# Two attention and gated-MLP layers on one core: engines held free ahead of the last chunks' chain, and the plan's price of narrow matmuls

## Chip, core and metric

One core of a Trainium2 chip. The kernel is one program; its time is the device time in microseconds of that core, as the median of several executions. The engines are TensorE (PE), VectorE (DVE), ScalarE (ACT), GpSimd (POOL) and SyncE (SP), each with its own instruction stream, which it works through in order, waiting on semaphores.

## What is computed

Two layers with the same weights over x of shape 2048 x 512, bfloat16:

```python
x = A_x
for _ in range(2):
    x = x + attention(layernorm(x))      # 32 heads of 16, one shared key and value head
    x = x + gated(layernorm(x))

# attention: q = x@wq (32 heads), k = x@wk, v = x@wv (16 columns each)
#            softmax(q k^T / 4) v, then @wo
# gated:     z = gelu(x@w_in)                      # 2048 x 1792
#            z1 = z[:, :896]; z2 = layernorm(z[:, 896:])
#            g = w_sp @ z2 + b_sp[:, None]         # w_sp is 2048 x 2048
#            (z1 * g) @ w_out
```

## The kernel before

**A plan made on the host.** The program is not written in the order in which it runs. Python code builds operations (`Op`: engine, duration in the plan, operations it depends on, priority) and a scheduler (`Sched`) plays them through in planned time; the order in which it commits them on each engine is the order of the instructions there. `_pick` chooses for an engine among the operations that are ready when it comes free, by priority; an operation that becomes ready a moment later is not considered, unless it comes from a stream with `grab`, which lets the engine stay idle for that long ahead of it. A result becomes visible some time after its end (`LAT`: 0.22 us from PE and ACT, 0.14 us from DVE, to readers on the same engine as well, except PE to PE). The waits of the program follow from the dependencies; nothing of the planned times is left in it but the order.

**Attention.** The 2048 queries come in chunks `[512, 512, 512, 256, 128, 128]` (`ci` 0 to 5). For each chunk and each set of four heads side by side there is a group of 16 units, one for each tile of 128 keys. A unit has four blocks of scores, 128 keys x 512. `FillStream` issues the score matmuls (qk, L1761) into PSUM in threes and twos by turns, `ExpStream` takes the exponential on ACT (L1428, output Pa, 128x1536 or 128x1024). A few blocks are computed on DVE instead (`DexStream`, L1615 to L1646, output Pd), in pairs of 1024. `SoloStream` places such a block by itself where PE would stand. `PVStream` multiplies with V (L1507). `WarmStream` issues matmuls on zeros (L1742) wherever the columns booked in the last 3.41 us of the plan fall below a bound; the columns of a job are its planned duration times a factor.

**The end of a chunk.** `finish_group` copies the group's result from PSUM (oT, L836), transposes it (for the last chunk on PE, else by DMA), takes the reciprocal of the softmax sums (L851) and normalises (on, L863). After the chunk's last group `project` transposes on, multiplies by wo (L943) and adds to X (L947). `mixer_chunk` takes the layer norm (st L638, mv L640, ve L642, POOL's rs L644, xn L653), transposes it (xnTB, L670 to L678), multiplies by w_in (L975 for the half z2, L1011 for z1), takes the gelu, and normalises z2 (st L1066, POOL's rs L1072, z2n L1076). Gelus are batched over chunks (0, 1), (2,), (3, 4), (5,), as ACT loads another table for them.

**The product with w_sp** runs over tiles of 128 rows s of z2 in passes: s 0 to 8 after chunk 1, 8 to 12 after chunk 2, 12 to 15 after chunk 4 (L1152 on PE, added up in gp by DVE, L1165). These jobs have low priority and fill gaps. The last tile, s = 15, is done after chunk 5 in `closing`: eight pieces of 256 rows; for each the product (L1211), a copy to E (DVE L1222 or ACT L1223), the addition of gp (L1226), the multiplication with z1 reloaded from DRAM (L1229), the product with w_out (L1244) and the addition to X (L1249). In layer 0 each piece is followed by the layer norm and the keys and values of layer 1, whose attention begins meanwhile; in layer 1 by the store.

**What a duration in the plan is.** `d_mm(n)` is the planned time of a matmul with n columns, `d_psum`, `d_sb` and `d_act` those of DVE and ACT operations. The lines that the change replaces:

```python
def d_mm(n):
    return max(n / 2400.0 + 0.006, min(0.045 + n * 0.43e-3, 0.155))
```

Of the kernel before, what the change touches and what calls it, by code (L numbers as in the profile page):

```python
# [6 lines left out]
BF16 = mybir.dt.bfloat16  # L7
# [25 lines left out]
class Op:  # L33
    __slots__ = ("eng", "fn", "dur", "deps", "prio", "seq", "start", "end", "vis", "sem", "val",
                 "clock", "unit", "job", "first", "nun", "users", "ready", "alts", "table", "lat", "dma", "at_commit", "cols", "slow")

# [21 lines left out]
class Sched:  # L58
# [3 lines left out]
    def __init__(self, side_banks):  # L62
        self.free = {e: 0.0 for e in ENGS}
        self.ready = {e: [] for e in ENGS}
        self.streams = {e: [] for e in ENGS}
        self.order = {e: [] for e in ENGS}
        self.commits = []
        self.banks = [Bank(b) for b in side_banks]
        self.seq = 0
        self.table = "exp"  # L70
        self.cache = {}
        self.nleft = 0
        self.exp_next = None
# [5 lines left out]
        self.full = False  # L79

    def lend(self, key, idxs, o):
# [34 lines left out]
    def op(self, eng, fn, dur, deps=(), prio=5.0, sem=None, job=None, first=False, alts=(), table=None,  # L116
           lat=None, dma=None, soft=(), cols=None, slow=None):
        o = Op()
        o.cols = dur * 2400.0 if cols is None else cols
        o.slow = dur * 2.0 if slow is None else slow  # L120
        o.eng = eng
        o.fn = fn
        o.dur = dur
        o.deps = []
        seen = set()
        for d in deps:
            if d is not None and id(d) not in seen:
# [24 lines left out]
        self.nleft += 1  # L152
        if o.nun == 0:
            self._arm(o)
        return o
# [13 lines left out]
    def _pick(self, eng):  # L169
# [3 lines left out]
        for o in self.ready[eng]:  # L173
            r = o.ready
            if o.first:
                r = max(r, bf)
            if o.eng != eng:
                dur = [d for e, _f, d in o.alts if e == eng][0]
                t0 = max(f, r)
                if self.exp_next is not None and self.exp_next() < t0 + dur:  # L180
                    continue
            if r < INF:
                late = o.unit is not None and o.unit < self.unit_now() + NEAR
                cands.append((r, 0.1 if late else o.prio, o.seq, o, 0.0))
        for st in self.streams[eng]:
# [98 lines left out]
    def job(self, pieces, cons, deps, prio, sem="side", piece_deps=None, soft=()):  # L284
# [3 lines left out]
        for i, (fn, dur) in enumerate(pieces):  # L288
            dd = list(deps) if i == 0 else [prev]
            if piece_deps is not None:  # L290
                dd += piece_deps[i]
            prev = self.op("pe", (lambda e, fn=fn: fn(e, j.bank.idx)), dur, dd, prio if i == 0 else min(prio, CONT), sem=sem, job=j,
                           cols=dur * 1900.0, first=(i == 0), soft=[d for c in cons for d in c.get("deps", ())] + list(soft) if i == 0 else ())
            if i == 0:
                self.first_op = prev
# [81 lines left out]
NEAR = 4  # L377
URGENT = 1.0
BACKLOG = 3.0
WARM = 1200.0  # L380
ENDX = 6
PR_LAST = 0.3
# [23 lines left out]
def d_mm(n):  # L406
    return max(n / 2400.0 + 0.006, min(0.045 + n * 0.43e-3, 0.155))


class Group:  # L410

    __slots__ = ("layer", "ci", "v", "t0", "n", "units", "q", "evac", "index", "pvb")

# [13 lines left out]
class Kern:  # L427
    def __init__(self, nc, A_x, A_wq, A_wk, A_wv, A_wo, B_x, B_w_in, B_w_sp, B_b_sp, B_w_out, out):
# [317 lines left out]
    def layer_groups(self, layer):  # L746
        t0 = 0
        for ci, n in enumerate(self.chunks):
            ns = 512 // n
            for s0, v in [(s, v) for s in range(0, 4, ns) for v in range(2)]:  # L750
                g = Group()
                g.layer, g.ci, g.v, g.t0, g.n = layer, ci, v, t0, n
                g.index = len(self.groups)
                g.pvb = self.pvb
# [76 lines left out]
    def finish_group(self, g, pv_last):  # L831
        sc = self.sc
        nq = g.n // 128
        par = self.evac_n % 2
        self.evac_n += 1
# [31 lines left out]
        onr = [d for qt in range(nq) for d in self.on_read[qt]]  # L867
        if g.ci < len(self.chunks) - 1:
            tr = self.transpose(self.oTt[:, par, :].rearrange("p (i r) -> p i r", i=4), self.oT[:, par, :],
# [7 lines left out]
            if g.v == 1 and g.q.s0 + g.q.ns == 4:  # L877
# [7 lines left out]
                 deps=[d for qt in range(nq) for d in self.on_read[qt]]) for h in hs],  # L885
            [ev, self.c_id], 0.9 if g.ci >= 3 else 1.2)
        m = ops[-1]
# [10 lines left out]
    def project(self, g, norms):  # L898
# [7 lines left out]
        for h in range((nq + 1) // 2):  # L906
# [15 lines left out]
            m = len(qts)  # L922
            if g.ci < 4:
                for qt in qts:
# [6 lines left out]
                alts=[("act", lambda e, b, cp=cp: e.activation(*cp(b), ACTF.Copy), d_act(m * 512) + 0.1)])],  # L931
                norms + [self.c_id], 0.9 if g.ci >= 3 else 1.3)
            for qt in qts:
# [3 lines left out]
        for qt in range(nq):  # L937
            t = g.t0 // 128 + qt

            def pe(e, b, qt=qt):  # L940
# [6 lines left out]
                fn=lambda e, b, t=t: e.tensor_tensor(self.X[:, t, :], self.b32(b)[:, 0:D], self.X[:, t, :], ALU.add),  # L947
                dur=d_psum(512), prio=0.8, deps=[self.x_op[t]])], [evs[qt], self.l_wo], 0.9 if g.ci >= 3 else 1.4)
            self.onT_read.append(pl)
# [4 lines left out]
    def mixer_chunk(self, g):  # L954
# [3 lines left out]
        T = [g.t0 // 128 + i for i in range(nt)]  # L958
        last = (g.ci == len(self.chunks) - 1)
        pr = PR_LAST if last else (PR_SMALL if g.ci >= 3 else 3.0)  # L960
        batch = [b for b in self.gelus if g.ci in b][0]
        evs = []
        war = list(self.xnTB_read)
        for i in range(0, nt, 2):
            ts = T[i:i + 2]
            evs += self.ln(ts, lambda t: [self.x_op[t]], self.xnTB[:, i:i + len(ts), :, :], war, pr, last, g.ci == 4)
        self.xnTB_read = []
# [25 lines left out]
        if last:  # L993
            z1v = self.z1L
            z1_war = list(self.dx_s.end)
        elif g.ci < batch[-1] < 3:
            z1v = self.gp[:, g.ci].bitcast(BF16)
            z1_war = [o for f in range(NF) for o in self.gp_read[(g.ci, f)]]
        else:
            z1v = self.z1s[:].rearrange("p (f t) -> p f t", f=NF)  # L1000
            z1v = z1v[:, :, 256:256 + n] if g.ci == 4 else z1v[:, :, 0:n]
            z1_war = list(self.z1s_free)
# [50 lines left out]
        for ci, (zt, zn, v) in zip(batch, zs):  # L1053
# [3 lines left out]
            if last:  # L1057
                self.z1L_spill = sp
            elif ci < batch[-1] < 3:
                for f in range(NF):  # L1060
                    self.gp_read[(ci, f)] = [sp]
            else:
                self.z1s_free = [sp] + (self.z1s_free if ci == 4 else [])
        ag = []
# [10 lines left out]
        for t in T:  # L1075
# [3 lines left out]
            self.z2_read[t] = []  # L1079
        for (s0, s1, ci) in self.passes:  # L1080
            if ci == g.ci:
# [367 lines left out]
class PVStream:  # L1449
# [10 lines left out]
    def peek(self, f):  # L1460
# [28 lines left out]
        if not u.last and self.u % 2 == 0:  # L1489
            nx = k.units[self.u + 1]  # L1490
            if any(x.unit is nx for x in k.dx_s.batch):
                k.dx_s.flush()
            if all(b.prod is not None and b.prod.start is not None for b in nx.blocks):
# [28 lines left out]
class DexStream:  # L1522
# [7 lines left out]
    def __init__(self, k):  # L1530
# [9 lines left out]
        self.last = []  # L1540
        self.gate = None

    def limit(self, layer):
# [114 lines left out]
class SoloStream:  # L1658
# [11 lines left out]
    def peek(self, f):  # L1670
        k = self.k
        sc = k.sc
        if self.x is None:
# [140 lines left out]
```

## Time and profile before

| | |
|---|---|
| median of 8 runs | 1823.95 us (1820.03 to 1826.98) |
| the profiled execution | 1820.03 us, span 1818.2 us |
| granted TensorE clock, mean | 0.998 |
| busy: ACT, DVE, PE, POOL | 1734.9, 1708.8, 1594.3, 50.7 us |
| exponentials on ACT (L1428) | 1431, 1622.0 us |
| matmuls on zeros (L1742) | 1111 |

The profile is of one execution. An engine's busy time counts its instructions, not its waits. A row of a timeline or of a group gives line, engine, operation, output <- inputs, shapes and count; behind it stands the idle time before it and what ended that. Layer 0 runs to about 945 us, where layer 1's attention has come up to its full rate; the last P·V of layer 0 ends at 864.2 us, that of layer 1 at 1763.9 us.

### The profile page before, as it was taken

How to read it: one execution, taken by the hardware profiler on the slowest of the kernel's cores; microseconds unless marked ns; L12 is line 12 of the kernel's file. 1: busy time of each engine (PE TensorE's matmuls, PEld its weight loads, DVE VectorE, ACT ScalarE, POOL GpSimd, SP SyncE). 2: the span in 40 equal slices, each digit the busy share in tenths (PEclk: the TensorE clock that was granted, in tenths of full speed). 3: DMA queues.
4: the chain of work that ended last, by engine and by line, in shares of the span. 5: the costliest groups of instructions: out<-in, count | busy, mean ns of one | idle time of the engine just before them, and what ended most of it. 6: DMA issues, size and time to landing. Idle time of an engine off the chain costs nothing.

```text
span 1818.2 us, 30022 instructions
## 1 busy us (share of the span) xinstructions
PE 1594.3 (88%) x11775; PEld 466.5 (26%) x11775; DVE 1708.8 (94%) x2947; ACT 1734.9 (95%) x1563; POOL 50.7 (3%) x90
## 2 busy tenths in 40 slices
PE   8888888888889999998888888888888999989998
PEld 3222222222222222232432222222222222222234
DVE  8999999999999999985999999999999999999878
ACT  7999999999999999999589999999999999999983
POOL 2000000000000000000010000000000000000000
PEclk9999999999999999999999999999999999999999
DMA  5353110011011020122220001100110111211113
GB/s 157 99 122 99 33 26 4 7 30 24 13 44 30 27 53 27 50 65 56 52 45 7 7 6 19 18 7 4 30 24 13 44 30 31 43 56 30 62 57 113
DMA packets 154517, 75.65 MB, mean 42 GB/s; under 512 B 108548, under 2 KB 150792, under 8 KB 154376
## 3 DMA queue, kind: packets, MB, share of 16 engines
q1 hardware_dynamic: 152792, 73.56, 16.0%
q8 instruction: 94, 1.54, 0.4%
q14 instruction: 47, 0.39, 0.1%
q10 hardware_dynamic: 1584, 0.16, 0.1%
HBM read 30.97 MB, written 17.83 MB: 27 GB/s over the span
## 4 chain that ended last, share of the span: by engine, by line
ACT 42%; DVE 21%; PE 18%; issue 17%; DMA 1%; POOL 0%; ACTq 0%; POOLq 0%; DVEq 0%
ACT Pa L1428 40%; PE ps_all L1761 5%; PE ps_all L1152 5%; PE ps_all L1507 3%; DVE E L1615 3%; DVE Pd L1646 3%; DVE E L1642 2%; DVE E L1644 2%; DVE E L1640 2%; PE ps_all L1244 1%; DVE st L638 1%; PE ps_all L1742 1%; DVE E L1643 1%; DVE gp L1165 1%; DVE st L1066 1%
## 5 line engine op out<-in xcount | busy, mean ns | idle before, releaser
L1428 ACT ACTIVATE Pa<-ps_all 128x1024 bf16<-128x1024 f32 (+1 forms) x1431 | 1622.0, 1383 | 16.0 <-PE ps_all L1761 13.1
L1761 PE MATMUL ps_all<-qs,kT 32*128 32x512 bf16 x4096 | 563.4, 385 | 181.7 <-ACT Pa L1428 163.9
L1615 DVE TENSOR_SCALAR E<-ps_all 128x512 f32<-128x512 f32 x528 | 358.7, 682 | 27.7 <-PE ps_all L1761 24.3
L1742 PE MATMUL ps_all<-zero 128*128 128x512 bf16 x1111 | 341.5, 388 | 15.7 <-DVE mv L1068 4.6
L1761 PEld LDWEIGHTS ps_all<-qs,kT 32*128 32x128 bf16 x4096 | 139.6, 91 | 759.4 <-ACT Pa L1428 717.5
L1646 DVE SCALAR_TENSOR_TENSOR Pd<-E 128x1024 uint16<-128x1024 f32 x265 | 321.6, 1213 | 4.4
L1507 PE MATMUL ps_all<-Pa,V 128*32 128x512 bf16 x3568 | 321.1, 385 | 0.0
L1152 PE MATMUL ps_all<-wsT,z2n 128*128 128x512 bf16 x714 | 203.2, 382 | 1.6 <-DVE X L947 0.7
L1642 DVE TENSOR_TENSOR E<-E 128x1024 f16<-128x1024 f16 x265 | 181.0, 683 | 4.5
L1507 PE MATMUL ps_all<-Pd,V 128*32 128x512 bf16 x528 | 184.8, 386 | 0.0
L1644 DVE TENSOR_TENSOR E<-E 128x1024 f16<-128x1024 f16 x265 | 180.8, 682 | 3.7
L1640 DVE TENSOR_SCALAR E<-E 128x1024 f16<-128x1024 uint16 x265 | 180.2, 680 | 1.2
L1742 PEld LDWEIGHTS ps_all<-zero 128*128 128x128 bf16 x1111 | 83.1, 98 | 192.6 <-issue 133.4
L1643 DVE TENSOR_SCALAR E<-E 128x1024 f16<-128x1024 f16 x265 | 110.4, 417 | 2.2
L1165 DVE TENSOR_TENSOR gp<-ps_all,gp 128x512 f16<-128x512 f32 x112 | 75.0, 683 | 24.1 <-PE ps_all L1152 23.9
L1507 PEld LDWEIGHTS ps_all<-Pa,V 128*32 128x32 bf16 x3568 | 63.9, 94 | 120.5 <-issue 113.4
L1152 PEld LDWEIGHTS ps_all<-wsT,z2n 128*128 128x128 bf16 x714 | 55.0, 97 | 93.3 <-issue 49.1
L975 PE MATMUL ps_all<-w_in_r,xnTB 128*128 128x448 bf16 x256 | 63.0, 355 | 4.6 <-DVE z2n L986 1.4
L1011 PE MATMUL ps_all<-xnTB,w_in_r 128*128 128x512 bf16 (+2 forms) x336 | 62.1, 310 | 1.1 <-DVE z1s L1022 0.6
L1244 PE MATMUL ps_all<-E 128*128 128x512 bf16 x224 | 54.1, 380 | 5.9 <-DVE E L1229 5.3
L642 POOL TENSOR_SCALAR ve<-mv 128x2 f32<-128x2 f32 (+1 forms) x28 | 9.8, 348 | 1381.2 <-DVE mv L640 1381.1
L836 DVE CAST oT<-ps_all 128x512 bf16<-128x512 f32 x64 | 43.7, 683 | 1.6 <-PE ps_all L1507 1.4
(87 smaller groups left out, 921.1 us busy)
## 6 DMA issues: line engine op xcount, KB each, us to landing
wsT_scratch<-gp SPq DMA_DIRECT2D x16, 512.0 KB, 3.6
wsT<-wsT_scratch SPq DMA_DIRECT2D x8, 1024.0 KB, 5.3
z1s<-z_scratch SPq DMA_DIRECT2D x16, 448.0 KB, 3.8
wsT<-wsT_scratch SPq DMA_DIRECT2D x8, 512.0 KB, 3.7
z_scratch<-z1s SPq DMA_DIRECT2D x4, 896.0 KB, 5.2
X<-in_A_x_dram SPq DMA_DIRECT2D x8, 256.0 KB, 5.9
out_dram<-X SPq DMA_DIRECT2D x16, 128.0 KB, 1.9
w_in_r<-in_B_w_in_dram SPq DMA_DIRECT2D x1, 1792.0 KB, 10.0
```

The source lines that it names most:

```text
L1152: ins = e.matmul(self.b32(b), self.z2n[:, s, f * 128:(f + 1) * 128], w_[:, s - s0, :] if s - s0 < na or not spare else wsp[:, s - s0 - na, :],
L1165: return e.tensor_tensor(dst, self.b32(b), dst, ALU.add)
L1428: return e.activation(k.Pa[:, base:base + n, :], k.b32(b0, n).rearrange("p (k q) -> p k q", k=n), ACTF.Exp, scale=SCALE)
L1507: ins = e.matmul(k.b32(u.grp.pvb)[32 * j:32 * j + 32, :], k.V[:, u.kt, 32 * j:32 * j + 32], b.slot, tile_position=(0, 32 * j), start=u.fir ...
L1615: c = k.sc.op("dve", lambda e: e.tensor_scalar(k.ey[:, s, 512 * i:512 * (i + 1)], k.b32(j.bank.idx)[:, 0:512], E_LOG2, E_BIAS, op0=ALU.mul ...
L1640: o2 = sc.op("dve", lambda e: e.tensor_scalar(x, lo, E_X * 2.0 ** -16, E_X * E_A, op0=ALU.mult, op1=ALU.add), d_sb(n, 0.521e-3), self.ops ...
L1642: o3 = sc.op("dve", lambda e: e.tensor_tensor(w, x, x, ALU.mult), d_sb(n, 0.521e-3), [o2, self.wfree], pr)
L1643: o4 = sc.op("dve", lambda e: e.tensor_scalar(w, w, E_C, None, op0=ALU.add), d_sb(n, 0.26e-3), [o3], pr)
L1644: o5 = sc.op("dve", lambda e: e.tensor_tensor(w, w, x, ALU.mult), d_sb(n, 0.521e-3), [o4], pr)
L1646: o7 = sc.op("dve", lambda e: e.scalar_tensor_tensor(po.bitcast(U16), y, E_D, w, op0=ALU.add, op1=ALU.add), d_sb(n, 1.042e-3), [o5] + self ...
L1742: return e.matmul(k.b32(pvb if b is None else b.idx), k.zero[:], k.zero[:, None, :].to_broadcast([P, 4, P]), start=b is not None, stop=b i ...
L1761: return e.matmul(self.b32(bank), self.kT[32 * j:32 * j + 32, g.v, kt * 128:(kt + 1) * 128], self.qs[32 * j:32 * j + 32, g.q.slot, :], til ...
```

## The change

Four edits. (1) Each operation gets a `grab` of its own, taken from `Sched.rush` at the time it is made, and `_pick` uses it as it uses that of streams: the engine may stay idle for up to 0.3 us ahead of such an operation. `rush` is 0.3 from `finish_group` of the second group (v = 1) of the last two chunks through `mixer_chunk` up to the statistics and normalisation of z2, and 0 elsewhere. (2) `d_mm` becomes n/2400 + 0.003 us, at least 0.026: for 128 columns 0.056 instead of 0.100, for 256 0.110 instead of 0.155, for 448 0.190 instead of 0.193, for 512 0.216 instead of 0.219. The columns booked for a job become its duration times 2300 instead of 1900. (3) Chunks, passes and gelu batches are lists by layer, with the same values for both, and the tests on the chunk's number count from the end (`fin`). (4) While `SoloStream` holds a block that it has taken and not yet placed, no batch of DVE blocks is closed and none taken.

```diff
@@ Sched.op / _pick
+        o.grab = self.rush
...
-                cands.append((r, 0.1 if late else o.prio, o.seq, o, 0.0))
+                cands.append((r, 0.1 if late else o.prio, o.seq, o, o.grab))
@@ Sched.job
-                           cols=dur * 1900.0, first=(i == 0), ...
+                           cols=dur * 2300.0, first=(i == 0), ...
@@
+RUSH = 0.3
...
 def d_mm(n):
-    return max(n / 2400.0 + 0.006, min(0.045 + n * 0.43e-3, 0.155))
+    return max(n / 2400.0 + 0.003, 0.026)
@@ Kern.__init__
-        self.chunks = [512, 512, 512, 256, 128, 128]
-        self.passes = [(0, 8, 1), (8, 12, 2), (12, 15, 4)]
-        self.gelus = [(0, 1), (2,), (3, 4), (5,)]
+        self.chunks = [[512, 512, 512, 256, 128, 128]] * 2
+        self.passes = [[(0, 8, 1), (8, 12, 2), (12, 15, 4)]] * 2
+        self.gelus = [[(0, 1), (2,), (3, 4), (5,)]] * 2
@@ finish_group
         nq = g.n // 128
+        sc.rush = RUSH if g.fin <= 1 and g.v == 1 else 0.0
@@ mixer_chunk, ahead of the passes
+        sc.rush = 0.0
@@ PVStream.peek (twice)
+                if k.dx_s.hold:
+                    return None
                 k.dx_s.flush()
@@ DexStream.take
-        if sc.bank_free() > t:
+        if self.hold or sc.bank_free() > t:
@@ SoloStream.peek / commit
+            k.dx_s.hold = True
...
+        k.dx_s.hold = False
```

The number of instructions stays nearly as it is. By the two orders of instructions, a few blocks of scores go to DVE instead of ACT (exponentials of 1536: 704 instead of 707, of 1024: 726 instead of 724; pairs of DVE blocks: 265 instead of 263), and there are 1066 matmuls on zeros instead of 1111.

More of the change, by code (lines that the diff above doesn't have):

```diff
@@ L34 @@
     __slots__ = ("eng", "fn", "dur", "deps", "prio", "seq", "start", "end", "vis", "sem", "val",
-                 "clock", "unit", "job", "first", "nun", "users", "ready", "alts", "table", "lat", "dma", "at_commit", "cols", "slow")
+                 "clock", "unit", "job", "first", "nun", "users", "ready", "alts", "table", "lat", "dma", "at_commit", "cols", "slow", "grab")
 class Job:
@@ L79, in __init__ @@
         self.full = False
+        self.rush = 0.0
     def lend(self, key, idxs, o):
@@ L292, in job @@
             prev = self.op("pe", (lambda e, fn=fn: fn(e, j.bank.idx)), dur, dd, prio if i == 0 else min(prio, CONT), sem=sem, job=j,
-                           cols=dur * 1900.0, first=(i == 0), soft=[d for c in cons for d in c.get("deps", ())] + list(soft) if i == 0 else ())
+                           cols=dur * 2300.0, first=(i == 0), soft=[d for c in cons for d in c.get("deps", ())] + list(soft) if i == 0 else ())
             if i == 0:
@@ L406, in d_mm @@
 def d_mm(n):
-    return max(n / 2400.0 + 0.006, min(0.045 + n * 0.43e-3, 0.155))
+    return max(n / 2400.0 + 0.003, 0.026)
 class Group:
-    __slots__ = ("layer", "ci", "v", "t0", "n", "units", "q", "evac", "index", "pvb")
+    __slots__ = ("layer", "ci", "fin", "v", "t0", "n", "units", "q", "evac", "index", "pvb")
 class QSet:
@@ L747, in layer_groups @@
         t0 = 0
-        for ci, n in enumerate(self.chunks):
+        for ci, n in enumerate(self.chunks[layer]):
             ns = 512 // n
@@ L752, in layer_groups @@
                 g.layer, g.ci, g.v, g.t0, g.n = layer, ci, v, t0, n
+                g.fin = len(self.chunks[layer]) - 1 - ci
                 g.index = len(self.groups)
@@ L867, in finish_group @@
         onr = [d for qt in range(nq) for d in self.on_read[qt]]
-        if g.ci < len(self.chunks) - 1:
+        if g.fin:
             tr = self.transpose(self.oTt[:, par, :].rearrange("p (i r) -> p i r", i=4), self.oT[:, par, :],
@@ L885, in finish_group @@
                  deps=[d for qt in range(nq) for d in self.on_read[qt]]) for h in hs],
-            [ev, self.c_id], 0.9 if g.ci >= 3 else 1.2)
+            [ev, self.c_id], 0.9 if g.fin <= 2 else 1.2)
         m = ops[-1]
@@ L922, in project @@
             m = len(qts)
-            if g.ci < 4:
+            if g.fin > 1:
                 for qt in qts:
@@ L931, in project @@
                 alts=[("act", lambda e, b, cp=cp: e.activation(*cp(b), ACTF.Copy), d_act(m * 512) + 0.1)])],
-                norms + [self.c_id], 0.9 if g.ci >= 3 else 1.3)
+                norms + [self.c_id], 0.9 if g.fin <= 2 else 1.3)
             for qt in qts:
@@ L947, in project @@
                 fn=lambda e, b, t=t: e.tensor_tensor(self.X[:, t, :], self.b32(b)[:, 0:D], self.X[:, t, :], ALU.add),
-                dur=d_psum(512), prio=0.8, deps=[self.x_op[t]])], [evs[qt], self.l_wo], 0.9 if g.ci >= 3 else 1.4)
+                dur=d_psum(512), prio=0.8, deps=[self.x_op[t]])], [evs[qt], self.l_wo], 0.9 if g.fin <= 2 else 1.4)
             self.onT_read.append(pl)
@@ L958, in mixer_chunk @@
         T = [g.t0 // 128 + i for i in range(nt)]
-        last = (g.ci == len(self.chunks) - 1)
-        pr = PR_LAST if last else (PR_SMALL if g.ci >= 3 else 3.0)
-        batch = [b for b in self.gelus if g.ci in b][0]
+        last = g.fin == 0
+        pr = PR_LAST if last else (PR_SMALL if g.fin <= 2 else 3.0)
+        batch = [b for b in self.gelus[g.layer] if g.ci in b][0]
         evs = []
@@ L965, in mixer_chunk @@
             ts = T[i:i + 2]
-            evs += self.ln(ts, lambda t: [self.x_op[t]], self.xnTB[:, i:i + len(ts), :, :], war, pr, last, g.ci == 4)
+            evs += self.ln(ts, lambda t: [self.x_op[t]], self.xnTB[:, i:i + len(ts), :, :], war, pr, last, g.fin == 1)
         self.xnTB_read = []
@@ L995, in mixer_chunk @@
             z1_war = list(self.dx_s.end)
-        elif g.ci < batch[-1] < 3:
-            z1v = self.gp[:, g.ci].bitcast(BF16)
+        elif g.ci < batch[-1] <= self.passes[g.layer][0][2]:
+            z1v = self.gp[:, g.ci].bitcast(BF16)[:, :, 0:n]
             z1_war = [o for f in range(NF) for o in self.gp_read[(g.ci, f)]]
@@ L1000, in mixer_chunk @@
             z1v = self.z1s[:].rearrange("p (f t) -> p f t", f=NF)
-            z1v = z1v[:, :, 256:256 + n] if g.ci == 4 else z1v[:, :, 0:n]
+            z1v = z1v[:, :, 256:256 + n] if g.fin == 1 else z1v[:, :, 0:n]
             z1_war = list(self.z1s_free)
@@ L1058, in mixer_chunk @@
                 self.z1L_spill = sp
-            elif ci < batch[-1] < 3:
+            elif ci < batch[-1] <= self.passes[g.layer][0][2]:
                 for f in range(NF):
@@ L1062, in mixer_chunk @@
             else:
-                self.z1s_free = [sp] + (self.z1s_free if ci == 4 else [])
+                self.z1s_free = [sp] + (self.z1s_free if g.fin == 1 else [])
         ag = []
@@ L1079, in mixer_chunk @@
             self.z2_read[t] = []
-        for (s0, s1, ci) in self.passes:
+        sc.rush = 0.0
+        for (s0, s1, ci) in self.passes[g.layer]:
             if ci == g.ci:
@@ L1491, in peek @@
             if any(x.unit is nx for x in k.dx_s.batch):
+                if k.dx_s.hold:
+                    return None
                 k.dx_s.flush()
@@ L1541, in __init__ @@
         self.gate = None
+        self.hold = False
     def limit(self, layer):
```

## Prediction

> **What bounds the kernel now.** I read the page first (busy shares, then the chain that ended last), then busy time by stretch, then the DVE and PE timelines where a layer ends.
>
> ```profile
> PE 1594.3 (88%) x11775; PEld 466.5 (26%) x11775; DVE 1708.8 (94%) x2947; ACT 1734.9 (95%) x1563; POOL 50.7 (3%) x90
> ACT 42%; DVE 21%; PE 18%; issue 17%; DMA 1%; POOL 0%; ACTq 0%; POOLq 0%; DVEq 0%
> ```
>
> ```profile
> 100.00:800.00 700.00, 613.90 (x4558) 166.76 (x4554) 674.59 (x1112) 697.33 (x604) 12.83 (x18) 1.00 0.17 42
> 864.00:880.00 16.00, 13.91 (x98) 7.32 (x95) 13.30 (x27) 5.16 (x9) 1.10 (x2) 1.00 0.01 3
> 880.00:945.00 65.00, 55.67 (x429) 25.53 (x426) 62.87 (x166) 46.51 (x65) 8.08 (x16) 1.00 0.29 67
> 1764.00:1781.00 17.00, 15.18 (x103) 8.16 (x102) 14.15 (x29) 5.50 (x10) 1.10 (x2) 1.00 0.04 8
> ```
>
> The columns are span, then PE, PEld, DVE, ACT and POOL busy, clock, DMA. Three regimes. In a layer's attention (100 to 800) ACT is busy 697.3 of 700 us: time there is the sum of its exponentials. DVE has 25.4 us to spare. When a layer's last chunk ends (864 to 880, 1764 to 1781) ACT is two thirds idle: one chain crosses PE, DVE, ACT and POOL. In the closing (880 to 945) DVE is busy 62.9 of 65.
>
> The chain on DVE after the last P·V of layer 0:
>
> ```profile
> 869.28 0.69 DVE L947 TENSOR_TENSOR X<-ps_all,X 128x512 bf16<-128x512 f32 x1 [0.60 <-PE ps_all L943]
> 869.89 0.68 DVE L1165 TENSOR_TENSOR gp<-ps_all,gp 128x512 f16<-128x512 f32 x1
> 870.49 0.68 DVE L638 BATCH_NORM_STATS2 st<-X 128x6 f32<-128x512 bf16 x1
> 871.09 0.67 DVE L1165 TENSOR_TENSOR gp<-ps_all,gp 128x512 f16<-128x512 f32 x1
> 871.68 0.17 DVE L640 BATCH_NORM_AGGREGATE mv<-st 128x2 f32<-128x6 f32 x1
> 871.77 0.66 DVE L1165 TENSOR_TENSOR gp<-ps_all,gp 128x512 f16<-128x512 f32 x1
> 872.34 0.14 DVE L642 TENSOR_SCALAR ve<-mv 128x1 f32<-128x1 f32 x1
> 872.40 1.27 DVE L1165 TENSOR_TENSOR gp<-ps_all,gp 128x512 f16<-128x512 f32 x2
> 873.60 0.40 DVE L653 TENSOR_SCALAR xn<-X,mv,rs 128x512 bf16<-128x512 bf16 x1
> ```
>
> Between X, st, mv and ve stands one gp addition each (L1165, work of the spatial pass that nobody needs yet). The plan believes that a result is visible to its own engine only 0.14 us after its end, so it fills that gap with a 0.6 us job; on the chip st starts where the gp addition ends, so the filler is pure delay.
>
> **Narrow matmuls in the plan.**
>
> ```profile
> 876.67 1.73 PE L1011 MATMUL ps_all<-xnTB,w_in_r 128*128 128x128 bf16 x28
> ```
>
> Less the last one's own 0.22 us (its row's mean), 1.51/27 = 56 ns from start to start. The plan booked 100 ns before, 56 ns now, so it moves towards the trace. For 512 columns it booked 219 ns, now 216; 9 matmuls in 1.94 us (chain, 1765.54) are 216. No instruction gets faster; only the order follows. "TensorE: Matmul & The Clock Gate" of the Trainium skill (Back-to-back issue gap) speaks against this: a stream of weight loads and matmuls sustains about 81 ns at 128 columns. By that the new plan would book 28 of them 0.7 us short, so that two chains could lose 1.4 us of their gain; the row has the same kind of stream at 56.
>
> **The order after, step by step.** I compare the two orders of instructions.
>
> *Layer 0's chain.* Gone are the gp additions between reciprocal and on (0.56 us), X and st (0.60), st and mv (0.60), mv and ve (0.57); of two behind ve one stays, and xn, whose rs was ready at 873.11, no longer waits until 873.60 (0.45). DVE alone would give 2.8. PE stands in the way: 5 pass matmuls between the transposes of oT and of on (7 before), then 4 before wo (5). At 0.216 each, from 865.4, on's transposes come at 866.5 (866.92 before), wo at 867.6 (868.22): 0.6 gained. X, st, mv, ve, rs and xn then end at about 871.1. PE now has 14 pass matmuls behind wo: 867.6+0.9+3.0 = 871.5, so xn's transposes start there instead of at 874.06: 2.55. After them 4 more (0.86 us) beside ACT's xnTB copy (0.60): w_in at 872.6 against 875.14. Behind xn stand 5 gp additions instead of 3: 871.1+3.0 = 874.1, just ahead of z2n's statistics (876.69-2.5). One gp lands in the 0.49 us hole ahead of the first E copy: +0.1. Net -2.4.
>
> *Layer 1's chain.* Same edits: 0.35 at the reciprocal (2 gp ahead, now 1), then 0.54, 0.60, 0.60, 0.57, 0.45. PE: 4 between the transposes (9), 5 before wo (6): wo at 1767.5 against 1768.84 to 1769.0 (-1.5). Behind wo 15 instead of 23: 1768.4+3.2 = 1771.6 for xn's transposes against 1774.68. The rest follows: -3.0. Four additions that lay behind the last oT now lie ahead of it (15 to 11), where DVE has holes (1.25, 0.81, 1.21 us behind L1152). Both chains: -5.4.
>
> *ACT's sum.* Counts in the orders: layer 0 has 356 exponentials of 1536 (357) and 357 of 1024; layer 1 has 348 (350) and 369 (367). A pair of one each takes 2.27 us (16 in 18.20), one of 1024 0.92 (31 in 28.60), so one of 1536 1.35. -1.35 and -2.70+1.84 = -0.86: -2.2 us. DVE takes one chain pair more per layer: 0.6 x 5 + 0.33 + 1.23 = 4.6 us by the rows' spacing, against 25.4 us spare in 100 to 800. Nothing, if the holes can be used; 9.2 us if they can't.
>
> *Closing.* Layer 0's: DVE gets one E copy and one qs copy more (0.6 each) and two V copies less (0.28 each), +0.65, where it has 2 us spare: 0 to +0.7, I take +0.5. Layer 1's: one E copy more, near a 0.92 us wait for PE: 0 to +0.6, +0.2.
>
> *Holding ACT.* The mark also sits on copies that ACT may take and on the last gelu batches: ACT may wait up to 0.3 us for them, with the exponentials (whose P·V and fills wait on ACT) queued behind. Four such places: 0 to +1.2, +0.4.
>
> *The clock.* 45 filler matmuls fewer (1111 to 1066).
>
> ```profile
> 515.00:520.00 5.00, 4.59 (x26) 0.98 (x24) 3.72 (x7) 4.62 (x5) 2.64 (x2) 0.71 0.76 253
> 840.00:845.00 5.00, 4.12 (x21) 0.96 (x22) 1.36 (x3) 4.00 (x4) 0.60 (x1) 0.66 0.98 280
> ```
>
> The granted clock fell twice, each time after a gelu batch, and ACT lost 0.38 and 1.00 us. The same page (HAM oscillation) wants only gaps over about 3.4 us avoided; here no PE idle around 840 exceeds 1.56 us and the clock fell, so the row decides. Six gelu batches: from both falls gone (-1.4) to four more (+4). I take 0, since the fillers beside the batches number about the same (35+4 against 8+27, 35 against 30; 16 and 14 against 19 and 17).
>
> *At nothing:* the per-layer lists of chunks (same values), the hold flag (it postpones a flush while a unit is being taken), SP's order (w_out's load goes behind two z1 reloads in layer 0, at 842; first used at 883) and POOL's. If w_out came late, the first L1244 would wait (an 896 KB transfer takes 5.2 us to land in the page's list); 40 us cover it.
>
> Sum: -5.4 - 2.2 + 0.5 + 0.2 + 0.4 = **-6.5 us**. The profiled execution took 1820.03 us (span 1818.2), the lowest of eight; its own time becomes 1813.5. The median, 3.9 higher, becomes 1823.95 - 6.5 = **1817.5**.
>
> **Rivals.**
> 1. *The closing swallows it.* DVE's work behind layer 0's last P·V is unchanged (12 gp instead of 13, but two copies more), so only its idle can shrink; 2.7 of 16 us there is idle. If layer 0's chain gives nothing and the re-planned ramp costs as much as the ACT blocks bring, layer 1's 3.0 less 0.5 remains: -2.5, 1821.5. For it: 62.9 of 65. Against it: the chain ends before that stretch begins.
> 2. *Slower: DVE becomes the bound in attention.* Its two extra pairs find no hole; each late Pd holds P·V, Pa slots stay taken, ACT waits. +9.2 in place of -2.2: -5.4+9.2+1.1 = +4.9, 1828.9. It decides once over 8 of the 9.2 us become ACT waits. For it: DVE 96%. Against it: 25 us of holes in each attention.
> 3. *Fillers:* four more falls of the clock, +4: about -2.5, as rival 1.
>
> **How the numbers follow.** What a measurement here can tell from no change is 0.2%, 3.6 us. Forecast 0.70 (nearly all of it beyond 3.6), rivals 1 and 3 0.20, rival 2 0.10. Faster 0.70, same 0.21, slower 0.09. Range: below, both falls gone, no holds, no price for the closings: -6.5-1.4-0.4-0.7 = -9.0, 1815; above, rivals 1 and 3 with 0.2 more in the ramp and 0.8 more at the holds, -1.5, 1822.5, leaving out rival 2. The eight runs lie up to 3.9 from their median, so a median of a few moves by some 2.5: 1812.5 to 1825.
>
> **What would show it.** Right: X, st, mv, ve back to back on DVE in both layers; from the last P·V's end to z2n normalised 15.5 us before in layer 0, about 13 after, and 15.9 to about 13 in layer 1; ACT's sum 2 us less with waits as before. Wrong: chains short but the stretch to layer 1's first full exponential as long as before (rival 1); new ACT waits on P·V in 100 to 800 (rival 2); more than two stretches below clock 1.00 (rival 3).

## The result, and the profile after

| | before | after |
|---|---|---|
| median | 1822.75 us (47 runs, 1818.16 to 1830.09) | 1813.77 us (17 runs, 1810.36 to 1815.88) |
| ratio | | 0.9949 [0.994, 0.9959] |
| profiled execution, its span | 1820.03, 1818.2 us | 1813.73, 1811.9 us |
| granted clock: profiled execution, mean of the timed ones | 0.998, 0.995 | 0.994, 0.995 |

The change saves 9.0 us by the medians and 6.3 between the two profiled executions. The one profiled execution of before was among its quicker ones, at a higher clock than its mean; the one of the change stands at its median. The forecast was -6.5.

Of the page of the changed kernel: the busy times, the chain that ended last, and the exponentials.

```profile
PE 1589.1 (88%) x11730; PEld 462.9 (26%) x11730; DVE 1719.9 (95%) x2962; ACT 1732.5 (96%) x1561; POOL 48.5 (3%) x90
...
ACT 41%; DVE 24%; PE 17%; issue 16%; DMA 1%; POOL 0%; ACTq 0%; POOLq 0%
...
L1434 ACT ACTIVATE Pa<-ps_all 128x1024 bf16<-128x1024 f32 (+1 forms) x1430 | 1619.7, 1374 | 17.5 <-PE ps_all L1774 15.9
```

The exponentials are 2.3 us shorter (1622.0 before). Busy shares hardly moved: such a change is not to be seen there. It is to be seen on DVE where layer 0 ends (columns: start, duration, operation):

```profile
867.65 0.69 DVE L952 TENSOR_TENSOR X<-ps_all,X 128x512 bf16<-128x512 f32 x1
868.37 0.69 DVE L641 BATCH_NORM_STATS2 st<-X 128x6 f32<-128x512 bf16 x1
869.10 0.18 DVE L643 BATCH_NORM_AGGREGATE mv<-st 128x2 f32<-128x6 f32 x1
869.32 0.15 DVE L645 TENSOR_SCALAR ve<-mv 128x1 f32<-128x1 f32 x1
869.39 0.68 DVE L1171 TENSOR_TENSOR gp<-ps_all,gp 128x512 f16<-128x512 f32 x1
870.14 0.41 DVE L656 TENSOR_SCALAR xn<-X,mv,rs 128x512 bf16<-128x512 bf16 x1
870.47 3.07 DVE L1171 TENSOR_TENSOR gp<-ps_all,gp 128x512 f16<-128x512 f32 x5
```

X, st, mv and ve now follow one another, one gp addition stands behind ve, and five behind xn, as the order had said. From the start of X to the start of xn it is 2.49 us; it was 4.32. In layer 1 the same four start at 1765.61, 1766.34, 1767.07 and 1767.28 us, with nothing between them either.

Busy time by stretch (span, then PE, PEld, DVE, ACT, POOL, then clock, DMA share, GB/s), with the stretches cut at the same places in the work:

```profile
100.00:800.00 700.00, 611.31 (x4539) 166.51 (x4537) 676.32 (x1112) 695.34 (x602) 12.92 (x18) 1.00 0.17 41
863.00:877.00 14.00, 13.31 (x101) 6.98 (x94) 12.76 (x27) 6.04 (x11) 1.10 (x2) 1.00 0.05 10
877.00:940.00 63.00, 56.25 (x419) 24.51 (x417) 62.64 (x165) 44.01 (x61) 8.19 (x16) 1.00 0.27 67
1761.00:1775.00 14.00, 12.66 (x96) 7.03 (x93) 12.56 (x26) 4.88 (x10) 1.10 (x2) 1.00 0.04 9
```

The stretch around the chain at a layer's end is 14 us long instead of 16 and 17. In attention ACT is busy 2 us less of 700 than before (695.34 against 697.33): it waits more there (4.0 us against 2.0).

The whole span, cut at four marks per layer in the timelines of ACT and DVE (us; "lag" from the end of the last full exponential, taken as the start of the table load behind it, to the copy of oT, "chain" from there to the first copy of E on DVE, "closing" from there to layer 0's last addition to X):

| | attention 0 | lag | chain | closing | attention 1 | lag | chain | tail | span |
|---|---|---|---|---|---|---|---|---|---|
| before | 863.24 | 1.02 | 15.90 | 54.38 | 828.68 | 0.75 | 16.82 | 37.41 | 1818.2 |
| after | 862.68 | 0.75 | 13.32 | 53.83 | 828.96 | 1.58 | 13.62 | 37.16 | 1811.9 |
| difference | -0.56 | -0.27 | -2.58 | -0.55 | +0.28 | +0.83 | -3.20 | -0.25 | -6.3 |

So the two chains carry nearly all of the difference between the two profiles, and the attention carries none of it, though its exponentials are shorter by 2.3 us.

### The profile page after: what moved, and what is told of

Its sections match the earlier page's. It is cut to its first block, busy times and chain, and to the rows that moved or that the text cites. A ratio compares the mean times of both kernels' runs of the same rounds, so it can differ in the third digit from the quotient of the medians.

```text
span 1811.9 us, 29980 instructions
## 1 busy us (share of the span) xinstructions
PE 1589.1 (88%) x11730; PEld 462.9 (26%) x11730; DVE 1719.9 (95%) x2962; ACT 1732.5 (96%) x1561; POOL 48.5 (3%) x90
## 4 chain that ended last, share of the span: by engine, by line
ACT 41%; DVE 24%; PE 17%; issue 16%; DMA 1%; POOL 0%; ACTq 0%; POOLq 0%
ACT Pa L1434 39%; PE ps_all L1774 5%; DVE E L1626 4%; PE ps_all L1158 4%; PE ps_all L1517 3%; DVE Pd L1657 3%; DVE E L1653 2%; DVE E L1651 2%; DVE E L1655 2%; DVE st L641 2%; PE ps_all L1250 1%; PE ps_all L1755 1%; DVE gp L1171 1%; DVE E L1654 1%; DVE xn L656 1%
## 5 line engine op out<-in xcount | busy, mean ns | idle before, releaser
L1434 ACT ACTIVATE Pa<-ps_all 128x1024 bf16<-128x1024 f32 (+1 forms) x1430 | 1619.7, 1374 | 17.5 <-PE ps_all L1774 15.9
L1626 DVE TENSOR_SCALAR E<-ps_all 128x512 f32<-128x512 f32 x532 | 361.3, 682 | 25.3 <-PE ps_all L1774 22.2
L1755 PE MATMUL ps_all<-zero 128*128 128x512 bf16 x1066 | 325.5, 390 | 16.9 <-ACT z1s L1047 3.1
L1657 DVE SCALAR_TENSOR_TENSOR Pd<-E 128x1024 uint16<-128x1024 f32 x267 | 324.0, 1213 | 4.3
L1653 DVE TENSOR_TENSOR E<-E 128x1024 f16<-128x1024 f16 x267 | 182.4, 683 | 4.7
L1651 DVE TENSOR_SCALAR E<-E 128x1024 f16<-128x1024 uint16 x267 | 181.9, 681 | 1.6
```

The source lines that it names most:

```text
L1434: return e.activation(k.Pa[:, base:base + n, :], k.b32(b0, n).rearrange("p (k q) -> p k q", k=n), ACTF.Exp, scale=SCALE)
L1626: c = k.sc.op("dve", lambda e: e.tensor_scalar(k.ey[:, s, 512 * i:512 * (i + 1)], k.b32(j.bank.idx)[:, 0:512], E_LOG2, E_BIAS, op0=ALU.mul ...
L1651: o2 = sc.op("dve", lambda e: e.tensor_scalar(x, lo, E_X * 2.0 ** -16, E_X * E_A, op0=ALU.mult, op1=ALU.add), d_sb(n, 0.521e-3), self.ops ...
L1653: o3 = sc.op("dve", lambda e: e.tensor_tensor(w, x, x, ALU.mult), d_sb(n, 0.521e-3), [o2, self.wfree], pr)
L1657: o7 = sc.op("dve", lambda e: e.scalar_tensor_tensor(po.bitcast(U16), y, E_D, w, op0=ALU.add, op1=ALU.add), d_sb(n, 1.042e-3), [o5] + self ...
L1755: return e.matmul(k.b32(pvb if b is None else b.idx), k.zero[:], k.zero[:, None, :].to_broadcast([P, 4, P]), start=b is not None, stop=b i ...
```

## The experiments

My theory was the forecast: holding shortens the chains, the rest is small. The rivals were that the durations and the booked columns do the work (they change the order everywhere), or the clock does. Twelve experiments were run. "Hold" is `RUSH = 0.3`, "price" the new `d_mm`, "booking" 2300 against 1900 columns per us, and `WARM` the bound below which matmuls on zeros are added (1200 before and after). The changed kernel is the base of every diff unless another is named; so each kernel but `before_w16` has edits (3) and (4) of the change as well. Each ratio is against the kernel before, timed beside it on the same chip.

**1. Hold without price and booking** (`rush_only`)

```diff
-                           cols=dur * 2300.0, ...
+                           cols=dur * 1900.0, ...
-    return max(n / 2400.0 + 0.003, 0.026)
+    return max(n / 2400.0 + 0.006, min(0.045 + n * 0.43e-3, 0.155))
```

> Engines hold themselves free as in the change; the plan's price of matmuls and the booked columns are the old ones. Theory (the filler additions inside the two last chains are the cost): the DVE order behind both last P.V is again X, st, mv, ve in a row, so from oT to the first E copy 13.3 us in layer 0 and 13.6 in layer 1 instead of 15.9 and 16.8; chains -5.5 us, one exponential of 1536 less -1.4; in all 5 to 8 us faster than the kernel before, at least two thirds of the change's 9. Rival (the plan's price of matmuls brings it): within 3 us of the kernel before.

1823.64 us, 0.9995 [0.9979, 1.001]: nothing gained that this comparison tells, against the 5 to 8 us expected. The chains were as short as expected, 13.89 and 13.32 us. The time was lost elsewhere; attention 1 took 838.5 us instead of 828.7. The windows of this kernel, where layer 1's attention begins (same columns):

```profile
945.00:950.00 5.00, 5.00 (x23) 0.92 (x23) 3.62 (x6) 3.66 (x5) 0.00 (x0) 0.50 0.00 0
950.00:955.00 5.00, 5.00 (x24) 0.88 (x20) 4.83 (x8) 3.93 (x5) 0.00 (x0) 0.50 0.00 0
955.00:960.00 5.00, 5.00 (x28) 0.74 (x20) 1.56 (x2) 3.98 (x4) 0.00 (x0) 0.50 0.01 3
960.00:965.00 5.00, 5.00 (x26) 0.82 (x23) 3.07 (x5) 3.48 (x5) 0.00 (x0) 0.50 0.00 2
```

The clock is at half for all of these 20 us, PE has no free moment, and ACT is busy 15.0 of 20 us: 5 us are lost in this place, about half of what attention 1 took longer. Over its twelve executions the mean clock ranged from 0.986 to 0.998, and the span from 1826.6 (at 0.986) to 1812.6 (at 0.998).

**2. Price and booking without hold** (`price_only`)

```diff
-RUSH = 0.3
+RUSH = 0.0
```

> The plan's new price of narrow matmuls and the new booking of columns alone, no holding (0 instead of 0.3). Theory: the fillers stand in both chains as before (gp between X, st, mv and ve), 9 pass matmuls between the transposes of oT and on, the same count of exponentials as before: chains within 1 us of 15.9 and 16.8, time within 3 us of the kernel before. Rival (price): 6 us faster or more. Second rival (the plan's order is a throw of dice whatever is edited): 3 us or more in either direction with unchanged chains.

1822.03 us, 0.9999 [0.999, 1.0009]. Both chains took 17.04 us. DVE's timeline in layer 0 shows the gp additions in their old places:

```profile
869.84 0.69 DVE L952 TENSOR_TENSOR X<-ps_all,X 128x512 bf16<-128x512 f32 x1 [0.60 <-PE ps_all L948]
870.45 0.68 DVE L1171 TENSOR_TENSOR gp<-ps_all,gp 128x512 f16<-128x512 f32 x1
871.05 0.68 DVE L641 BATCH_NORM_STATS2 st<-X 128x6 f32<-128x512 bf16 x1
871.65 0.67 DVE L1171 TENSOR_TENSOR gp<-ps_all,gp 128x512 f16<-128x512 f32 x1
```

So price and booking alone neither move the fillers nor the time. This kernel differs from the change in `RUSH` alone: with the hold, lags and chains together fall from 35.4 to 29.3 us and the median from 1822.03 to 1813.77, at mean clocks of 0.9957 and 0.9945 (each timed beside the kernel before: ratios 0.9999 and 0.9949).

**3. Hold at the last chunk alone** (`rush_last`)

```diff
-        sc.rush = RUSH if g.fin <= 1 and g.v == 1 else 0.0
+        sc.rush = RUSH if g.fin == 0 and g.v == 1 else 0.0
```

> As the change, but the hold is set for the last chunk alone (fin 0), not for the last two. Theory: the last chunk's chain is what ends the layer, so the gain stays within 2 us of the change's 9: chains of 13.3 and 13.6 us. Rival (chunk 4's steps coming earlier, so that the third pass starts earlier, is what pays): half of the gain or less, with more additions left behind the last oT and longer chains.

1815.41 us, 0.9962 [0.9949, 0.9974]; chains 13.31 and 14.84 (in layer 1 ACT makes the first copy of E here, 13.7 us after oT). As expected: the last chunk is what matters, and the last but one adds nothing that this comparison tells.

**4. Hold for DVE's operations alone** (`rush_dve`)

```diff
-        o.grab = self.rush
+        o.grab = self.rush if eng == "dve" else 0.0
```

> As the change, but only DVE's operations are marked; PE, ACT and POOL hold nothing. Theory: the DVE fillers are gone, so X, st, mv and ve stand in a row, but more pass matmuls stand on PE between the transposes (6 and 6 instead of 5 and 4) and ahead of wo (6 instead of 4 and 5): chains 0.5 us longer than the change's, time 0.5 to 3 us slower than the change and 5 to 8 faster than the kernel before. Rival (holding PE and ACT is what pays): within 3 us of the kernel before.

1819.94 us, 0.9981 [0.9972, 0.9991]; chains 14.09 and 14.42. The gain is 3.1 us, less than expected, though the chains keep most of theirs. The rest of the span is 1785.9 (1783.7 before).

**5 to 7. The clock, with more matmuls on zeros** (`before_w16` on the kernel before; `rush_only_w16` on `rush_only`; `warm1600` on the change)

```diff
-WARM = 1200.0
+WARM = 1600.0
```

> The kernel before with more filler matmuls: the bound on booked columns is 3060+1600 instead of 3060+1200 in 3.41 us (1324 fillers instead of 1111); the chains keep their gp additions. Over its executions the kernel before takes about 1.2 us more for each 0.001 of granted clock that it lacks (0.9952 on average, 0.998 in the profiled one). Theory (half-clock stretches cost it some 5 us on average): clock 0.998 or more, 3 to 5 us faster than the kernel before, chains as before (15.9 and 16.8 us). Rival (the clock only goes along with something else, or fillers cost PE as much as they save): within 1 us of it, or slower.

> Holding alone with the old price and booking, and the raised bound (1310 fillers). Theory (holding alone shortens the chains by 5 us, and rush_only lost that again to a clock of 0.9907): clock 0.997 or more, 4 to 7 us faster than before_w16 and 8 to 11 faster than the kernel before; chains 13.3 to 13.9 us. Rival (what rush_only lost has to do with its order in the attention, not with the clock): no more than 2 us faster than before_w16.

> The change with the raised bound (1258 fillers instead of 1066). Theory: its half-clock stretches (clock 0.9945 on average, some 5 us) mostly go: clock 0.997 or more, 2 to 5 us faster than the change, 11 to 14 faster than the kernel before; 5 to 9 faster than before_w16. Rival (fillers cost as much as they save): within 1 us of the change.

| | matmuls on zeros | mean clock | chains | median | ratio |
|---|---|---|---|---|---|
| before, 1600 | 1324 | 0.998 | 17.26, 17.26 | 1822.69 | 1.0002 [0.9991, 1.0013] |
| hold, 1600 | 1310 | 0.998 | 13.91, 13.28 | 1817.12 | 0.9966 [0.9951, 0.998] |
| change, 1600 | 1258 | 0.998 | 13.32, 13.31 | 1811.11 | 0.9942 [0.9923, 0.996] |

The first row against the second has the same old price, the same booking and the same clock; beside the hold, only edits (3) and (4) differ. Holding brings 5.6 us, as expected (4 to 7). The two profiles differ by 5.7 in span; their lags and chains together differ by 6.2 (36.46 against 30.22), the rest of the span is 1783.1 and 1783.7. The kernel before gains nothing from the raised bound, which missed the expectation: between its two profiles, both near full clock, its lags and chains grow by 2.0 us (34.49 to 36.46) and the rest shrinks by 0.6. The change gains 2.7 by the medians. That is the lowest median of all, but the two kernels were not timed beside each other and their intervals overlap, so the step from the change to this version isn't shown.

**8. Hold and booking, old price** (`rush_book`)

```diff
-    return max(n / 2400.0 + 0.003, 0.026)
+    return max(n / 2400.0 + 0.006, min(0.045 + n * 0.43e-3, 0.155))
```

> Holding and the new booking of columns (2300), but the old durations of matmuls in the plan (100 ns at 128 columns). With the old durations the new booking counts 230 columns for a matmul of 128, 23% more than rush_only's 190, so that fewer fillers stand there (1062). Theory (what the new price is worth is fillers that stand where the clock needs them): clock no better than rush_only's 0.9907, time within 3 us of rush_only's. Rival (booking alone is what helps the change): clock 0.994 or more, 6 us faster than the kernel before or more.

1825.16 us, 1.0014 [0.9999, 1.0029], chains 13.63 and 13.28, and again the half clock, for 17.1 us from 946.4: like the first experiment, as expected.

**9. The change again** (`change_again`), as an anchor for the three that follow.

> The change once more, as the yardstick beside the three others of this call. Both theories: 1812 to 1816 us, 7 to 11 faster than the kernel before.

1814.42 us, 0.9954 [0.9942, 0.9967]; chains 13.31 and 13.64.

**10. The change with still more matmuls on zeros** (`after_w20`)

```diff
-WARM = 1200.0
+WARM = 2000.0
```

> The change with the bound on booked columns raised to 3060+2000 (1452 fillers instead of 1066; as many exponentials and DVE pairs as in the change). Theory (half-clock stretches cost the change some 4 us, fillers cost little where the chains hold PE free): clock 0.998 or more, 1 to 5 us faster than the change. Rival (fillers in the way of the exponentials' score matmuls cost as much as the clock brings, as in before_w16): within 1 us of the change or slower.

1815.91 us, 0.9961 [0.9948, 0.9973], with 1452 of them: by the medians 1.5 slower than the change timed beside it, which the intervals do not tell from no difference. A gain of 1 to 5 us did not come, as the rival said, though the mean clock rose (0.997). That PE's added work takes what the clock brings fits this, but isn't shown by itself.

**11. Hold and price, old booking** (`book1900`)

```diff
-                           cols=dur * 2300.0, ...
+                           cols=dur * 1900.0, ...
```

> Holding and the new durations of matmuls, with the old booking of columns (1900; 1142 fillers). Theory (the durations, not the booking, are what the holding needs beside it: the plan's narrow matmuls behind the last P.V and in the ramp of layer 1 stand where PE is really free): ramp and chains as in the change, clock 0.994 or more, within 3 us of the change. Rival (the booking): like rush_only, within 3 us of the kernel before.

1821.04 us, 0.999 [0.9981, 0.9999], chains 13.72 and 13.72, but 1787.8 us in the rest of the span. That the price suffices was a miss: neither price nor booking does it alone beside the hold.

**12. No hold, but a plan that lets DVE read its own results at once** (`dve_lat0`). This removes the reason for the fillers instead of forbidding them.

```diff
-        o.ready = max([d.end if d.eng == "pe" and o.eng == "pe" else ...
+        o.ready = max([d.end if d.eng == o.eng and o.eng in ("pe", "dve") else ...
-RUSH = 0.3
+RUSH = 0.0
```

> No holding; instead the plan lets DVE read its own result at once (0 instead of 0.14 us), with the new price and booking. Theory (the fillers stand in the chain only because of the 0.14 us): X, st, mv, ve stand in a row in layer 0 without any holding, so its chain from oT to the first E copy takes 13 us or less. But the plan now finds room for 290 pairs of score blocks on DVE instead of 265 and 27 exponentials of 1024 fewer on ACT (25 us). 25 pairs of 4.6 us are 115 us, more than the 100 us that DVE has idle, so DVE becomes the bound: 5 to 30 us slower than the change. Rival (DVE does run dependent operations back to back, so the plan is truer and the room is there): 10 us faster than the change or more.

2073.39 us, 1.1374 [1.1353, 1.1396]: 250 us slower, far outside what I expected. The plan now sets dependent steps of the pairs on DVE (L1651 to L1657) directly behind each other more often (742 times, 430 in the kernel before), and gives DVE 289 pairs of 1024 instead of 265. ACT's longest waits in this kernel (us in total, times, longest):

```profile
ACT Pa L1434 <- PE ps_all L1774: 139.7, 180, 3.8
ACT E L1229 <- PE ps_all L1217: 134.3, 8, 40.4
```

And its DVE in attention:

```profile
402.26 0.69 DVE L1651 TENSOR_SCALAR E<-E 128x1024 f16<-128x1024 uint16 x1
402.98 0.69 DVE L1653 TENSOR_TENSOR E<-E 128x1024 f16<-128x1024 f16 x1
403.59 1.28 DVE L1626 TENSOR_SCALAR E<-ps_all 128x512 f32<-128x512 f32 x2
```

L1653 reads what L1651 wrote and starts 0.72 us after it. L1626, which doesn't depend on L1653, starts 0.61 after that. Over this trace L1653 starts 720 ns (median) after L1651 where it follows directly (212 times); where another operation follows L1651, that starts after 608 ns (78 times). In the kernel before it is 720 ns (130 times) and 602 ns (135 times). So a dependent step on DVE does start about 0.12 us later than an independent one. The plan's 0.14 is about right, and a plan that denies it falls behind at 742 steps by 0.12 us each, 89 us in all.

That alone does not make 250 us. X, st, mv and ve do stand in a row here without any hold (from X to xn 2.49 us in layer 0, as in the change), but the first half of the expectation missed: the two chains take 50.0 and 61.2 us. Of the 260 us that the profile is longer than the change's, 75 lie in the two attentions and 185 from the last full exponential of each layer to the end of its closing. There 298 and 339 matmuls of the pass stand behind the last oT, where the change has 33 and 32. So most of the loss is work with w_sp that was late and no longer fitted into the attention; that the missing 0.12 us made it late is likely but wasn't followed step by step.

**All runs together, at one clock.** Over all executions the span grows by 1.05 us for each 0.001 of mean clock lost (one slope fitted for all kernels, a constant for each). Extrapolated with it to clock 1.000, an estimate good to a few us (without the twelfth experiment):

| | hold | price | booking | WARM | mean clock | span at clock 1.000 |
|---|---|---|---|---|---|---|
| before | no | old | 1900 | 1200 | 0.9951 | 1816.1 |
| price_only | no | new | 2300 | 1200 | 0.9957 | 1815.8 |
| before_w16 | no | old | 1900 | 1600 | 0.9979 | 1818.7 |
| rush_only | yes | old | 1900 | 1200 | 0.9907 | 1811.2 |
| rush_book | yes | old | 2300 | 1200 | 0.9903 | 1812.5 |
| book1900 | yes | new | 1900 | 1200 | 0.9946 | 1813.8 |
| rush_only_w16 | yes | old | 1900 | 1600 | 0.9984 | 1813.7 |
| rush_dve | DVE | new | 2300 | 1200 | 0.9940 | 1811.8 |
| rush_last | last | new | 2300 | 1200 | 0.9936 | 1807.5 |
| change | yes | new | 2300 | 1200 | 0.9945 | 1806.1 |
| warm1600 | yes | new | 2300 | 1600 | 0.9983 | 1807.9 |
| after_w20 | yes | new | 2300 | 2000 | 0.9972 | 1811.2 |

Three things stand in it. No kernel without hold is below 1815; every one with it is between 1806 and 1814, and in each of them both lags and chains together are 28.9 to 30.2 us, against 34.5 to 36.5 without it. By this estimate the first experiment did gain 4.9 us and lost 4.6 to the clock (0.9951 to 0.9907). And matmuls on zeros cost 1.8 to 3.3 us for each 190 to 215 of them (four pairs of kernels), which would limit their use; each of these differences is within the estimate's own few us.

## Why the prediction was right, and where it wasn't

**The chains: right in mechanism and size.** -2.58 and -3.20 us against -2.4 and -3.0. From the last P·V's end to the start of z2n's normalisation it went from 15.0 to 12.4 us in layer 0 (to its end, as the prediction had it, from 15.5 to 12.9) and from 15.9 to 12.7 in layer 1. The experiments show that holding does this, with the old price (the first, and the sixth against the fifth) or the new (the change against the second).

**"The filler is pure delay": not quite.** A removed filler leaves the 0.12 us that the last experiment shows. In the timeline above, X to st is 0.72 us and st to mv 0.73, so X to xn shrank by 1.83 instead of the 0.60 + 0.60 + 0.57 + 0.45 = 2.22 that I counted. The plan's 0.14 us, which I took for an error, was the measured size. What the plan had wrong is to fill 0.14 with 0.6. The sum still came out, since PE stood in the way by less than I had estimated: xn's transposes were to wait 0.4 us for PE behind xn (871.5 against 871.1), and waited 0.06 (870.55 to 870.61 in the changed kernel).

**The lag in layer 1: left out, +0.83.** PE's timeline of the changed kernel just ahead of the last P·V:

```profile
1758.36 2.12 PE L1158 MATMUL ps_all<-z2n 128*128 128x512 bf16 x9
1760.40 0.61 PE L1517 MATMUL ps_all<-Pa,V 128*32 128x512 bf16 x8
```

The kernel before, at the same place:

```profile
1761.90 1.47 PE L1152 MATMUL ps_all<-z2n 128*128 128x512 bf16 x6
1763.30 0.61 PE L1507 MATMUL ps_all<-Pa,V 128*32 128x512 bf16 x8
```

In the changed kernel ACT's last full exponential had ended by 1759.54, but nine matmuls of the pass were queued ahead of the P·V that needed it, which started 0.86 us later; before, it started 0.08 us after the exponential's end (1763.22). I counted the pass matmuls between the chain's steps and not those ahead of its start. With layer 0's -0.27 this is +0.56.

**ACT's sum and holding ACT: the sum right, the saving not seen in one profile.** The exponentials took 2.3 us less (forecast 2.2). But both attentions together shrank by 0.28 only, since ACT's waits for score blocks rose from 3.8 to 4.3 us in layer 0's (40 to 860) and from 2.2 to 3.3 in layer 1's: +1.6, where I had +0.4 for holds. Most of them (5.0 of 7.6 us) lie not at the marked operations but in the steady attention, at the falls of the clock, one of 0.75 us just ahead of the first.

**The clock: rival 3 came by half.** The changed kernel's profile has four falls, 20.5 us at half clock in all, against two with 6.8 us. Two of its windows:

```profile
395.00:400.00 5.00, 3.19 (x20) 0.65 (x17) 4.93 (x8) 4.25 (x4) 0.00 (x0) 0.81 0.32 30
400.00:405.00 5.00, 5.00 (x25) 1.05 (x25) 4.63 (x9) 4.00 (x5) 0.00 (x0) 0.50 0.66 210
```

ACT is short by 0.75 and 1.0 us there. By my own sign ("more than two stretches below clock 1.00") that is the wrong side; but the medians don't show it, since before and after have nearly the same mean clock over their executions (0.9951 and 0.9945). I read "each time after a gelu batch" out of one execution with two falls; three of the four here (398, 1268 and 1320 us) lie behind no gelu batch, and other kernels' falls do not lie alike, so that reading is not supported.

**The closings: -0.55 and -0.25, where I had +0.5 and +0.2.** More copies on DVE were no burden. Rival 1 is out: what the chain gained, the closing did not take.

**DVE as the bound, rival 2: did not come.** There was no new wait on P·V in attention, and 676.3 of 700 us is still below the whole. In the twelfth experiment something like it came: DVE was busy 195.9 of 200 us (300 to 500) and ACT 190.9.

**The step from span to median.** I took the 3.9 us between the profiled execution and the median of eight as constant. It was not: before's execution had clock 0.998 against a mean of 0.995, and 0.003 of clock is some 3 us. So -6.3 between profiles became -9.0 between medians. That the -6.3 lies so near to my -6.5 is in part luck: the attention gave 0.3 us where I had 1.8, and the lags lost 0.6, but the closings and the chains gave more. The -9.0 is the lower end of my range, though not for the reasons that the range gave: the falls of the clock did not go. Added up at one clock, the measured terms are -5.78 for the chains, +0.56 for the lags, -2.3 for the exponentials and -0.8 for the closings, -8.3 in all, of 9.0 by the medians and 10.0 by the estimate at one clock; the remainder is in no term. My -6.5 was short of that in the closings (1.5) and the chains (0.4), with 0.4 of holds that can't be seen in the waits; the lags went against it.

**What is open.** By the estimate at one clock the change is 5.1 us below hold alone, while price and booking without hold give 0.3. Part of it may be the exponentials' -2.3, which the other plans share only in part (1622.5 us in the first experiment, 1621.7 in the third, 1620.6 in the eleventh, and 1620.9 in the second, without hold). Price and booking have to be there together, and I have no mechanism for that: each plan reorders all of the attention. The span beyond the lags and chains varies from 1779 to 1794 us from one profile to another, but much of that is the clock: brought to clock 1.000 by the same slope it is 1777 to 1778 in the four profiles of plans with price, booking and a hold on all engines at `WARM` 1200 or 1600, and 1781 to 1783 in all the others. So by this estimate some 3 to 5 us of the 9 to 10 are a gain in that rest, whose cause stays open. Nor was it settled why the clock, once down at 945 us, stayed at half for 20 us while PE was busy all the time. The Trainium skill ("TensorE: Matmul & The Clock Gate", What's actually happening) says that one busy window of about 3.4 us lifts the gate. The four windows of the first experiment, 5.00 of 5.00 busy at 0.50, do not agree, so there the measurement decides. And 1600 for `WARM` on the change may be worth another 2 to 3 us; its interval does not tell it from the change, and the estimate at one clock has it 1.8 us slower.

## What to carry to other kernels

Where a greedy scheduler fills a short, true latency on a critical chain with a long job, let it hold the engine for those few operations alone: that took 4 to 6 us out of the two layers' lags and chains in every plan tried, while a plan that denied the latency upset the whole kernel. After any edit to a plan compare stage by stage, and compare kernels at the same granted clock: the first experiment looked like no gain and, by the estimate at one clock, held a gain of 5 us. Before a profiled execution is set beside a median, see at what clock it ran.

## What the runs showed of the hardware

- On DVE a step that reads the one before it starts about 0.12 us later than one that doesn't (0.72 against 0.60 us for 128x1024 f16).
- PE's clock stayed at half for 20.5 us with PE busy throughout (first experiment, from 944.5 us), and an execution with 0.001 less mean clock took about 1 us of 1815 more.
- In every profile the stretches at half clock last 3.41 us or a whole multiple of it (two of 3.41 us before; 6.83, 3.41, 3.41 and 6.83 us after). In the 7 us ahead of the four falls after, PE's longest idle was 0.6 to 1.8 us.
- 28 matmuls of 128 columns, each with a weight load of its own, again took 1.73 us in the changed kernel, 56 ns from start to start at full clock; so the loss of 1.4 us that the prediction weighed against the new price did not come:

```profile
873.22 1.73 PE L1016 MATMUL ps_all<-xnTB,w_in_r 128*128 128x128 bf16 x28
```
